# Sums of the second weight matrix given out singly over the groups of the first layer's last two units, in a fused pooling-attention and snake-activation kernel

## The chip, the cores and the metric

The kernel runs on one core of a Trainium2 chip. The metric is the device time of one execution in microseconds (us); the median of three executions before the change is 909.51 us (908.82 to 912.5). A core has a matrix engine (PE, with its weight loads PEld), a vector engine (DVE), an activation engine (ACT), GpSimd (POOL) and a queue engine (SP) that issues most transfers. Each engine works through its own instructions in the order in which the program recorded them, and waits for the others by semaphores.

## The reference

The attention pools keys and values by 8 and gives `x` of 4608 tokens by 512. What the change touches is behind it:

```python
def _moe_ref(x, w_in, w_out, alpha):
    h = x @ w_in                       # 4608x512 @ 512x2048
    s = np.sin(alpha * h)
    g = h + s * s / (alpha + 1e-09)
    return (g @ w_out)                 # 4608x2048 @ 2048x512
```

All of it is in 32-bit floats.

## The kernel before

**Two layers, one behind the other.** The first layer (`h` and `g`) runs over 9 units `u` of 512 tokens. Units 0 to 6 lie under the attention; units 7 and 8 are made by `hidden_late`, without attention beside them. `g` goes out to a buffer in HBM (`g_bridge`). The second layer (`outputs`) runs over 8 batches of 576 tokens and reads `g` back with `load_g` (tiles r11, r12, r21, r22).

**Seven products in place of eight.** Both layers use a Strassen-Winograd scheme: a product of two 2x2 block matrices is made from seven block products of sums of blocks. In the first layer a unit has four groups J = 0 to 3 (256 columns of each half of `h`); a group accumulates its products in PSUM banks b1, b6, b5, b7 (the name tells which product is the last or the first in it). Products 1 and 5 of groups 1 to 3 are themselves made by a second level of the scheme. That is `late_chain`: steps a, b, d, e for product 1 (c1) and for product 5 (c5). They are made for the *next* group N, in eight pieces, put between the halves of this group's products by `chain()`. Step a has two matmuls and two ACT copies (L1083 and L1084); d has one matmul and a DVE sum (L1093); e has two matmuls that wait for that DVE sum. Behind c1.e, `copy(N.b6, N.b1)` on ACT seeds bank b6 of the next group, and the next group's first product accumulates on it.

**Order inside a group** (J of 1 and above, L1158 to L1221): ACT sine of the group before (from b7); product 6 with c1.a and c5.a; copy b7 <- b6; squares of the group before; product 2 with c1.b and c5.b; the DVE sums that finish the group before (`finish`, L1224, one of 512 and one of 1024 columns) and its store; product 7 with c1.d, DVE sum g11 (L1102), c5.d; sine of it; product 3 with c1.e, DVE sum g01 (L1102), c5.e; sine and square of g01; DVE sum g00; product 4; copy of b5 to the tile p5 (L1221). Group 0 has the same products, but its chain starts a product later, so c1.e and c5.e fall into product 4, *behind* the sine and the square of g01 on ACT.

**The second layer's weights.** `load_w_out` brings `w_out` in four transfers, copies its quarters into seven tiles wb1 to wb7 on GpSimd (`put`, L704), and makes the outer sums on DVE (L713: 16 instructions of 128x512, four for each pair of row blocks). `inner_w` makes the sums of the scheme's second level (L731: four of 128x512 for each product 4, 6, 1, 2, 7, 5, and later 3); results land in `we1`, `we2` (which until then hold first-layer chain weights), or in the column blocks of the first layer's own weights `A[1]`, `A[2]`, `A[3]` that are used up. All are due before the second layer's product that reads them; product 1 is the first, then 2, 4, 6, 7, 5, 3.

**Where these are put.** A list `x[slot]` of 28 slots per unit (seven per group) holds what is recorded at a slot (`extras(k)`). `load_w_out` is a generator; `next(w)` at slots 9 to 23 of unit 7 and 6 to 20 of unit 8 each record a whole block: four L713 sums, or the four (twice: eight) L731 sums of a product. `late_weights` makes the chain weights of group J on GpSimd (L795), `late_x` the sums of x (L1066). `outputs` is a generator too: its first `next(o)` records the four DVE sums of 128x576 (L1454) that make the first operands of the second layer, the second its first product, the third its second product with an ACT copy (L1627) and two more sums.

Of the kernel before, what the change touches and what calls it, by code (L numbers as in the profile page):

```python
# [19 lines left out]
P = 128  # L20
# [20 lines left out]
class Kernel:  # L41
# [637 lines left out]
    def load_w_out(self, wp):  # L679

        nc, h, kk = self.nc, self.DM // 2, self.K2 // 2
        src = self.w_out.rearrange("(k p) n -> p k n", p=P)
        self.W = {}
        self.wb = {p: wp.tile([P, self.NJ, 2, 2, P], F32, name=f"wb{p}") for p in range(1, 8)}
        self.we = {p: wp.tile([P, 3, 2, 2, P], F32, name=f"we{p}") for p in (1, 2)}
        flat = lambda t: t[:].rearrange("p a b c d -> p (a b) (c d)")
        b11, b21, b22, t4, t1, t2, b12 = (flat(self.wb[p]) for p in range(1, 8))

        raw = {}
        for k in range(0, kk, 4):
            for i in range(2):
                t = self.wb[5 + i] if k == 0 else self.gp.tile([P, self.NJ, JW, 2, self.T], F32, name=f"r1{i + 1}")
                x = t[:].rearrange("p a b c d -> p (a b c d)")[:, 0:4 * self.DM]
                raw[i, k] = x.rearrange("p (k j a n c) -> p k j a n c", k=4, j=2, a=4, n=2)
                nc.sync.dma_start(out=x.rearrange("p (k c) -> p k c", k=4), in_=src[:, i * kk + k:i * kk + k + 4, :])

        def put(i, k):

            for j, t in enumerate(((b11, b12), (b21, b22))[i]):
                yield
                for n in range(2):
                    nc.gpsimd.tensor_copy(out=t[:, k:k + 4, n * P:(n + 1) * P].rearrange("p k (a c) -> p k a c", a=4),  # L704
                                   in_=raw[i, k][:, :, j, :, n, :])
        yield from put(0, 0)
        yield from put(1, 0)
        for c in range(0, kk, 2):
            if c == 2:
                yield from put(0, 4)  # L710
            yield
            s = slice(c, c + 2)
            tt = lambda o, x, y: nc.vector.tensor_tensor(out=o[:, s], in0=x[:, s], in1=y[:, s], op=OP.subtract)  # L713
            tt(t1, b12, b11)
            tt(t2, b22, t1)
            tt(b12, b22, b12)

            tt(t4, b21, t2)
            if c == 2:
                yield from put(1, 4)  # L720
        for p in (4, 6, 1, 2, 7):
            yield
            self.inner_w(p, wp)
        yield

    def inner_w(self, p, wp):

        nc = self.nc
        x = self.wb[p]
        b = lambda i, j: x[:, :, i - 1, j - 1, :].rearrange("p (k j) d -> p k j d", k=2)  # L730
        tt = lambda o, x, y: nc.vector.tensor_tensor(out=o, in0=x, in1=y, op=OP.subtract)  # L731
        if p in (4, 6, 7, 5):
            J = (4, 6, 7, 5).index(p)
            t1, t2, t4 = (self.A[i][:, :, J * JW * P:(J + 1) * JW * P].rearrange("p k (j d) -> p k j d", j=2) for i in (1, 2, 3))
        else:
            e = self.we[p] if p in self.we else wp.tile([P, 3, 2, 2, P], F32, name=f"we{p}")
            t1, t2, t4 = (e[:, i] for i in range(3))
        steps = [lambda: tt(t1, b(1, 2), b(1, 1)), lambda: tt(t2, b(2, 2), t1),
                 lambda: tt(b(1, 2), b(2, 2), b(1, 2)), lambda: tt(t4, b(2, 1), t2)]
        self.W[p] = {1: b(1, 1), 2: b(2, 1), 3: b(2, 2), 4: t4, 5: t1, 6: t2, 7: b(1, 2)}  # L740
        if wp:
            for f in steps:
                f()
        return steps

# [44 lines left out]
    def sums(self, steps):  # L792

        for o, x, y, op in steps:
            self.nc.gpsimd.tensor_tensor(out=o, in0=x, in1=y, op=op)  # L795
# [240 lines left out]
    def late_tiles(self, u):  # L1036

        if u < self.NU - 1:
            t = self.home(0, [P, self.K1, 2 * TH])
            t = [t[:, i] for i in range(4)]  # L1040
            m5 = self.we[2][:].rearrange("p a b c d -> p (a b c d)")[:, 1024:1280]
        else:
            t = [self.gq.tile([P, self.NJ, self.T], F32, name=f"s{i}0")[:].rearrange("p a b -> p (a b)")[:, 0:4 * P] for i in range(4)]
            m5 = self.gq.tile([P, self.NJ, self.T], F32, name="s01")[:].rearrange("p a b -> p (a b)")[:, 0:2 * P]
        self.m5 = m5.rearrange("p (a b c) -> p a b c", a=2, b=1)
        self.x2 = t[:2]
        self.w3 = [x.rearrange("p (i m) -> p i m", i=4) for x in t[2:]]

    def late_weights(self, J, ps=(1, 5)):

        for p in ps:
            n = (1, 5).index(p)
            w = self.w3[n] if J == 3 else self.we[J][:].rearrange("p a b c d -> p (a b c d)")[:, n * 512:n * 512 + 512].rearrange("p (i m) -> p i m", i=4)
            A = self.A[p][:].rearrange("p k (J j m) -> p k J j m", j=2, m=P)[:, :, J]
            L = lambda i, j: A[:, j, i]
            s1, s2, s3, s4 = (w[:, i] for i in range(4))
            self.sums(((s1, L(1, 0), L(1, 1), OP.add), (s2, s1, L(0, 0), OP.subtract), (s3, L(0, 0), L(1, 0), OP.subtract), (s4, L(0, 1), s2, OP.subtract)))
            self.WL[p, J] = {1: L(0, 0), 2: L(0, 1), 3: s4, 4: L(1, 1), 5: s1, 6: s2, 7: s3}

# [39 lines left out]
    def hidden_late(self, u, extra):  # L1099
# [20 lines left out]
        for J in range(self.NJ):  # L1120
            def extras(k):
                for f in extra[7 * J + k]:
                    f()
# [39 lines left out]
            if N:  # L1163
                y = self.psum([P, 4, P], N.banks[1])
                c1, c5 = (self.late_chain(N, p, ps, y[:, i:i + 2], i == 0) for p, ps, i in ((1, N.b1, 0), (5, N.b5, 2)))
                steps = iter((c1.a, c5.a, c1.b, c5.b, c1.d, c5.d, c1.e, c5.e))

            def chain():
                f = next(steps, None)
                if f:  # L1170
                    f()
                if N and f is c1.e:
                    copy(N.b6[:], N.b1[:])
            halves = (0, 1), (2, 3)
            behind = J == 0
            extras(2)
            product(G, 6, G.b6, halves[0])
            if not behind:
                chain()
# [19 lines left out]
            product(G, 7, G.b7, halves[1])  # L1199
            add(G.g[:, 1, :, 1], G.b7[:], G.p5[:])  # L1200
            chain()
            sin(G, 1, 1, G.g[:, 1, :, 1])
            extras(5)
            product(G, 3, G.b6, halves[0])
# [1 line left out]
            product(G, 3, G.b6, halves[1])  # L1206
            add(G.g[:, 0, :, 1], G.b6[:], G.p5[:])
            chain()
            sin(G, 0, 1, G.g[:, 0, :, 1])
            square(G, 0, 1)  # L1210
            add(G.g[:, 0, :, 0], G.b1[:], G.s[:, 0, :, 0])
            extras(6)
            product(G, 4, G.b7, halves[0])
            if behind:
                chain()
            product(G, 4, G.b7, halves[1])
            if behind:
                chain()
            if N:
                N.p5 = self.tp.tile([P, JW, TH], F32, name="p5")  # L1220
                nc.vector.tensor_copy(out=N.p5[:], in_=N.b5[:])  # L1221
# [227 lines left out]
    def outputs(self):  # L1449
# [136 lines left out]
        for k in range(len(seq) + 1):  # L1586
# [47 lines left out]
            if last:  # L1634
                if k != 1:
                    second()
                third()
                if k == 5:
                    self.inner_w(3, self.gs)
                combine(last)  # L1640
            for _ in sums:
                pass
# [9 lines left out]
    def run(self):  # L1652
        nc, tc = self.nc, self.tc
        pool = lambda s, n, b, **kw: s.enter_context(tc.tile_pool(name=n, bufs=b, **kw))
        with ExitStack() as top:
# [10 lines left out]
            with ExitStack() as one:  # L1666
# [35 lines left out]
                for u in range(self.NU):  # L1702
                    x = self.carry(u)
                    if u == self.B - 1:
# [1 line left out]
                        wo = pool(top, "wo", 1, side="right")  # L1706
                        self.gp = pool(top, "gp", 1, side="right")
                        self.WL, self.XL = {}, {}
                        w = self.load_w_out(wp=wo)
                        next(w)  # L1710
                        self.late_tiles(u)
                        for i in (9, 10, 12, 13, 15, 16, 17, 18, 20, 21, 23):
                            x[i].append(lambda: next(w))
                        self.late_weights(1, (1,))
                        self.late_x(u, 1)
                        x[0].append(lambda: self.late_weights(1, (5,)))
                        x[1].append(lambda: self.late_x(7, 5, nc.vector))
                        x[4].append(lambda: self.late_weights(2))
                        x[6].append(lambda: self.late_weights(3))
                    elif u > self.B - 1:  # L1720
                        homes.close()
                        self.gq = pool(top, "gq", 1, side="right")
                        self.late_tiles(u)
                        for i in (6, 10, 14, 15, 17, 20):
                            x[i].append(lambda: next(w))
                        x[0].append(lambda: self.late_x(8, 1))
                        x[0].append(lambda: self.late_x(8, 5))
                        x[6].append(lambda: self.late_weights(3))
                        x[5].append(lambda: self.load_g(0, ("r11", "r12", "r22")))
                        for i, f in zip((23, 25, 25, 27), self.inner_w(5, None)):  # L1730
                            x[i].append(f)
                        o = self.outputs()
                        for i in (22, 25, 27):
                            x[i].append(lambda: next(o))
                    (self.hidden if u < self.B - 1 else self.hidden_late)(u, x)
                self.end_hidden()
# [41 lines left out]
```

## Time and profile before

| what | value |
|---|---|
| median of three executions | 909.51 us (908.82 to 912.5) |
| profiled execution, its own time | 911.08 us |
| span of its instructions | 909.3 us |
| granted TensorE clock | 0.999 |
| unit 7 (419.4 to 468.7 us) | 49.3 us |
| unit 8, with the first matmuls of the second layer (468.7 to 526 us) | 57.3 us |
| DVE busy in unit 7 / in 468.7 to 526 | 32.01 us / 46.70 us |
| POOL busy in unit 7 / in 468.7 to 526 | 22.02 us / 7.81 us |
| behind it (526 to 909.3 us) | second layer |

The profile's timeline lists instructions by start time; equal ones that follow each other are merged, so that "x4" with 1.03 us is the time of four matmuls together. In brackets stands the idle time of the engine ahead of the instruction and which engine's instruction ended it. Times in the text, such as 494.23, are us from the start of the span.

### The profile page before, as it was taken

The page shows a single profiled execution, that of the slowest core. Times are in us where ns is not written, and L with a number is a line of the kernel's source. Part 1 is how long each engine was busy: PE and PEld are TensorE (multiplying, and loading weights), DVE is VectorE, ACT ScalarE, POOL GpSimd, SP SyncE. Part 2 cuts the span into 40 slices and gives each one's busy share as a digit, 9 for nine tenths or more (in the row PEclk, how much of TensorE's full clock was granted, in tenths as well). Part 3 has the DMA queues.
Part 4 walks back from the last instruction along what each step waited for, and adds up shares of the span by engine and source line. Part 5 has one row for each costly group of instructions (what it writes and reads, how often), then busy time and mean ns, then how long its engine had stood idle before and what let it go on. Part 6 is the DMA issues. An engine that isn't in the chain of part 4 may idle for free.

```text
span 909.3 us, 18214 instructions
## 1 busy us (share of the span) xinstructions
PE 895.6 (98%) x7086; PEld 816.1 (90%) x7086; DVE 691.8 (76%) x1035; ACT 444.1 (49%) x1082; POOL 243.9 (27%) x276
## 2 busy tenths in 40 slices
PE   8999999999999999999999899999999999999997
PEld 5787888888888888888888799999999999999997
DVE  6675766758677685765577999979798888889894
ACT  5696685877768778687767621111121111111111
POOL 4788462824428253436330000000000000000000
PEclk9999999999999999999999999999999999999999
DMA  9956766759577595648136247161618162534401
GB/s 248 252 179 170 198 187 188 202 144 259 151 210 189 172 237 138 178 142 294 49 124 216 93 117 226 36 216 39 223 27 222 40 186 77 169 92 128 134 14 40
DMA packets 128749, 141.15 MB, mean 155 GB/s; under 512 B 46920, under 2 KB 95704, under 8 KB 128664
## 3 DMA queue, kind: packets, MB, share of 16 engines
q1 hardware_dynamic: 125880, 137.88, 53.2%
q10 hardware_dynamic: 2784, 2.11, 0.9%
q8 instruction: 56, 0.92, 0.5%
q14 instruction: 29, 0.24, 0.1%
HBM read 75.37 MB, written 47.19 MB: 135 GB/s over the span
## 4 chain that ended last, share of the span: by engine, by line
PE 91%; DVE 3%; ACT 2%; POOL 1%; DMA 1%; issue 1%; SPq 0%; DVEq 0%; POOLq 0%
PE PS L1499 42%; PE PS L835 33%; PE PS L1117 6%; PE PS L1015 3%; PE PS L308 2%; PE PS L600 2%; PE PS L1079 1%; PE PS L613 1%; DMA q<-in_q_dram 1%; POOL kvin L131 1%; DMA h<-in_k_dram 1%; ACT s L992 1%; DVE h L1224 1%; DVE h L1102 0%; ACT s L985 0%
## 5 line engine op out<-in xcount | busy, mean ns | idle before, releaser
L835 PE MATMUL PS<-home,a 128*128 128x256 f32 x848 | 199.9, 382 | 1.8 <-DVE h L810 1.3
L835 PEld LDWEIGHTS PS<-home,a 128*128 128x128 f32 x848 | 156.7, 190 | 28.7 <-issue 5.0
L835 PE MATMUL PS<-home,as 128*128 128x256 f32 x576 | 138.9, 383 | 0.0
L1499 PE MATMUL PS<-s,wb 128*128 128x144 f32 x896 | 119.2, 286 | 0.7 <-ACT PS L1627 0.7
L835 PEld LDWEIGHTS PS<-home,as 128*128 128x128 f32 x576 | 105.2, 190 | 14.8 <-ACT PS L811 1.2
L1549 POOL TENSOR_TENSOR cc<-cc,cb 128x576 f32<-128x576 f32 x1 | 2.0, 1980 | 423.2 <-DVE cb L1454 423.2
L1499 PEld LDWEIGHTS PS<-s,wb 128*128 128x128 f32 x896 | 113.6, 190 | 1.1 <-ACT PS L1627 1.1
L992 ACT ACTIVATE s<-s,c 128x256 f32<-128x256 f32 (+1 forms) x228 | 114.2, 565 | 0.0
L131 POOL TENSOR_TENSOR kvin<-kvin 96x768 f32<-96x768 f32 (+3 forms) x42 | 73.6, 1752 | 72.3 <-DMA kvin<-in_v_dram 70.6
L985 ACT ACTIVATE s<-h,al 128x256 f32<-128x256 f32 x144 | 65.5, 509 | 51.0 <-DVE h L810 30.5
L1627 ACT COPY PS<-PS 128x144 f32<-128x144 f32 x56 | 14.7, 263 | 144.3 <-PE PS L1499 141.7
L1499 PE MATMUL PS<-r,wb 128*128 128x144 f32 x512 | 73.2, 286 | 0.0
L1499 PE MATMUL PS<-s,a 128*128 128x144 f32 x512 | 73.2, 286 | 0.0
L810 DVE TENSOR_TENSOR h<-PS,p 128x512 f32<-128x512 f32 x56 | 38.1, 680 | 44.6 <-PE PS L835 28.3
L985 ACT ACTIVATE s<-PS,al 128x256 f32<-128x256 f32 x144 | 59.9, 467 | 16.0 <-PE PS L835 13.9
L1499 PEld LDWEIGHTS PS<-r,wb 128*128 128x128 f32 x512 | 67.1, 190 | 0.1
L1499 PEld LDWEIGHTS PS<-s,a 128*128 128x128 f32 x512 | 67.0, 190 | 0.0
L1224 DVE TENSOR_TENSOR h<-PS,s 128x512 f32<-128x512 f32 x36 | 24.7, 686 | 51.4 <-ACT s L992 51.4
L1647 ACT COPY PS<-PS 128x144 f32<-128x144 f32 x56 | 14.7, 263 | 88.0 <-PE PS L1499 88.0
L1224 DVE TENSOR_TENSOR h<-h,s 128x1024 f32<-128x1024 f32 x36 | 55.4, 1538 | 0.9 <-ACT s L992 0.9
L1499 PE MATMUL PS<-x,wb 128*128 128x144 f32 x384 | 54.9, 286 | 0.0
L1499 PE MATMUL PS<-s,we 128*128 128x144 f32 x384 | 54.9, 286 | 0.0
(274 smaller groups left out, 1662.7 us busy)
## 6 DMA issues: line engine op xcount, KB each, us to landing
g_bridge<-h SPq DMA_DIRECT2D x72, 512.0 KB
r<-g_bridge SPq DMA_DIRECT2D x31, 1152.0 KB
out_dram<-o SPq DMA_DIRECT2D x122, 72.0 KB
kvin<-in_k_dram SPq DMA_DIRECT2D x14, 576.0 KB
q<-in_q_dram SPq DMA_DIRECT2D x7, 1024.0 KB
kvin<-in_v_dram SPq DMA_DIRECT2D x14, 512.0 KB
aM<-tr SPq DMA_DIRECT2D x54, 92.0 KB
aM<-tr SPq DMA_DIRECT2D x54, 88.0 KB
```

The source lines that it names most:

```text
L131: self.nc.gpsimd.tensor_tensor(out=t[..., 0:w] if w > D else out, in0=t[..., 0:w], in1=t[..., w:2 * w], op=OP.add)
L308: nc.tensor.matmul(ps[e][r0 + r:r0 + r + q.shape[-1], h, :], q[s], kb[s, hp, :], start=True, stop=True)
L600: nc.tensor.matmul(o[r:r + 64], w, x, start=start and i < 2, stop=False, skip_group_check=True)
L810: add = lambda o, x, y: nc.vector.tensor_tensor(out=o, in0=x, in1=y, op=OP.add)
L835: nc.tensor.matmul(ps[:, jj, :], self.A[p][:, kk, f * P:(f + 1) * P], x[:, kk, :], start=(start and n == 0), stop=(kk == 1), skip_group_ch ...
L985: self.nc.scalar.activation(out=G.s[:, i, jj, j, :], in_=src[:, jj], func=AF.Sin, scale=self.al[:, f:f + 1])
L992: self.nc.scalar.activation(out=x, in_=x, func=AF.Square, scale=self.c[:, f:f + 1])
L1015: nc.tensor.matmul(o, W[m][:, G.J - J0], X[m], start=start and n == 0, stop=True, skip_group_check=True)
L1117: nc.tensor.matmul(ps[:, jj, :], self.A[p][:, kk, f * P:(f + 1) * P], x[:, kk, :], start=(start and n == 0), stop=(kk == 1), skip_group_ch ...
L1224: add = lambda o, x, y: self.nc.vector.tensor_tensor(out=o, in0=x, in1=y, op=OP.add)
L1499: nc.tensor.matmul(out, W[:, J // 2, J % 2, :], A[:, J, :], start=(start and J == 0), stop=(J == self.NJ - 1), skip_group_check=True)
L1627: nc.scalar.copy(out=x1[:, 0, :], in_=x0[:, 1, :])
```

## The change

- `load_w_out` no longer is a generator: it returns `put` and `sums`, and `inner_w` returns its four sums as functions. They are recorded one by one by a new `fill(n)` in `hidden_late`, which stands at three places of each group: n = 0 ahead of product 6, n = 1 behind c5.d (behind the sum g11, ahead of its sine), n = 2 at the end of product 4.
- The GpSimd copies `put` move up: the first half from slots 9 to 13 of unit 7 to slot 2, ahead of `late_weights(2)` (which moves from slot 4 to 3) and `late_weights(3)`; the second half to slot 6.
- The eight inner sums of products 1 and 2 go to GpSimd.
- In group 0 the sine and square of g01 are recorded behind the last two chain steps, and so behind the seed copy of b6 on ACT. In group 3 (no N), `extras(6)` moves ahead of that sine, and with it the ACT copy L1627.
- The first `next(o)` moves from slot 22 of unit 8 (group 3) to `fill(1)` of group 1. For this the tiles that lay in its way move: the chain's m5 into a used block of `A[5]`, unit 8's chain weights of group 3 into used blocks of `A[6]` and `A[7]`; `late_weights(3)` of unit 8 therefore waits for product 6 and 7 of group 0.

```diff
+        def sums(c):
             s = slice(c, c + 2)
-            tt = lambda o, x, y: nc.vector.tensor_tensor(...)
+            tt = lambda o, x, y: lambda: nc.vector.tensor_tensor(...)
+            return [tt(t1, b12, b11), tt(t2, b22, t1), tt(b12, b22, b12), tt(t4, b21, t2)]
+        return put, sums
...
-        tt = lambda o, x, y: nc.vector.tensor_tensor(out=o, in0=x, in1=y, op=OP.subtract)
+        eng = nc.gpsimd if p in (1, 2) else nc.vector
+        tt = lambda o, x, y: eng.tensor_tensor(out=o, in0=x, in1=y, op=OP.subtract)
...
+            self.m5 = self.A[5][:, :, 0:P].unsqueeze(2)
+            self.w3 = [self.A[i][:, :, 0:2 * P].rearrange("p k (j m) -> p k j m", j=2) for i in (6, 7)]
...
+            def fill(n):
+                for f in self.fillers[u, J, n]:
+                    f()
...
             extras(2)
+            fill(0)
             product(G, 6, G.b6, halves[0])
...
             add(G.g[:, 1, :, 1], G.b7[:], G.p5[:])
             chain()
+            fill(1)
             sin(G, 1, 1, G.g[:, 1, :, 1])
...
             add(G.g[:, 0, :, 1], G.b6[:], G.p5[:])
             chain()
-            sin(G, 0, 1, G.g[:, 0, :, 1])
-            square(G, 0, 1)
+            if not N:
+                extras(6)
+            if not behind:
+                sin(G, 0, 1, G.g[:, 0, :, 1])
+                square(G, 0, 1)
             add(G.g[:, 0, :, 0], G.b1[:], G.s[:, 0, :, 0])
-            extras(6)
+            if N:
+                extras(6)
             product(G, 4, G.b7, halves[0])
...
             if behind:
                 chain()
+                sin(G, 0, 1, G.g[:, 0, :, 1])
+                square(G, 0, 1)
+            fill(2)
...
+                        x[2] += [lambda: put(0, 0), lambda: put(1, 0)]
+                        x[3].append(lambda: self.late_weights(2))
                         x[6].append(lambda: self.late_weights(3))
+                        x[6] += [lambda: put(0, 4), lambda: put(1, 4)]
+                        self.fillers[7, 1, 0] = sums(0) + sums(2)[:2]
+                        self.fillers[7, 1, 1] = sums(2)[2:]
+                        self.fillers[7, 2, 0] = sums(4)
+                        self.fillers[7, 3, 0] = sums(6)
...
+                        w = {p: self.inner_w(p, q) for p, q in ((1, self.we[1]), (2, self.we[2]), (4, 0), (6, 1), (7, 2), (5, 3))}
                         o = self.outputs()
+                        F = self.fillers
+                        F[8, 0, 2] = w[4]
+                        F[8, 1, 0] = w[1] + w[6][:1]
+                        F[8, 1, 1] = w[6][1:3] + [lambda: next(o)]
+                        F[8, 2, 0] = w[6][3:] + w[2] + w[7][:1]
+                        F[8, 2, 1] = w[7][1:3]
+                        F[8, 3, 0] = w[7][3:] + w[5][:1]
+                        F[8, 3, 1] = w[5][1:3]
+                        F[8, 3, 2] = w[5][3:]
```

More of the change, by code (lines that the diff above doesn't have):

```diff
@@ L701, in put, with inner_w @@
             for j, t in enumerate(((b11, b12), (b21, b22))[i]):
-                yield
                 for n in range(2):
                     nc.gpsimd.tensor_copy(out=t[:, k:k + 4, n * P:(n + 1) * P].rearrange("p k (a c) -> p k a c", a=4),
[L705 to L711, printed above, removed]
-            s = slice(c, c + 2)
[L713 to L726, printed above, removed]
+                                          in_=raw[i, k][:, :, j, :, n, :])
+        def sums(c):
+            s = slice(c, c + 2)
+            tt = lambda o, x, y: lambda: nc.vector.tensor_tensor(out=o[:, s], in0=x[:, s], in1=y[:, s], op=OP.subtract)
+            return [tt(t1, b12, b11), tt(t2, b22, t1), tt(b12, b22, b12), tt(t4, b21, t2)]
+        return put, sums
+    def inner_w(self, p, parts):
         nc = self.nc
@@ L730, in inner_w @@
         b = lambda i, j: x[:, :, i - 1, j - 1, :].rearrange("p (k j) d -> p k j d", k=2)
-        tt = lambda o, x, y: nc.vector.tensor_tensor(out=o, in0=x, in1=y, op=OP.subtract)
-        if p in (4, 6, 7, 5):
-            J = (4, 6, 7, 5).index(p)
-            t1, t2, t4 = (self.A[i][:, :, J * JW * P:(J + 1) * JW * P].rearrange("p k (j d) -> p k j d", j=2) for i in (1, 2, 3))
-        else:
[L736 to L739, printed above, removed]
+        eng = nc.gpsimd if p in (1, 2) else nc.vector
+        tt = lambda o, x, y: eng.tensor_tensor(out=o, in0=x, in1=y, op=OP.subtract)
+        if isinstance(parts, int):
+            t1, t2, t4 = (self.A[i][:, :, parts * JW * P:(parts + 1) * JW * P].rearrange("p k (j d) -> p k j d", j=2) for i in (1, 2, 3))
+        else:
+            t1, t2, t4 = (parts[:, i] for i in range(3))
         self.W[p] = {1: b(1, 1), 2: b(2, 1), 3: b(2, 2), 4: t4, 5: t1, 6: t2, 7: b(1, 2)}
[L741 to L744, printed above, removed]
+        return [lambda: tt(t1, b(1, 2), b(1, 1)), lambda: tt(t2, b(2, 2), t1),
+                lambda: tt(b(1, 2), b(2, 2), b(1, 2)), lambda: tt(t4, b(2, 1), t2)]
     def bank(self, shape, i=None):
@@ L1042, in late_tiles @@
         else:
-            t = [self.gq.tile([P, self.NJ, self.T], F32, name=f"s{i}0")[:].rearrange("p a b -> p (a b)")[:, 0:4 * P] for i in range(4)]
-            m5 = self.gq.tile([P, self.NJ, self.T], F32, name="s01")[:].rearrange("p a b -> p (a b)")[:, 0:2 * P]
+            t = [self.gq.tile([P, self.NJ, self.T], F32, name=f"s{i}1")[:].rearrange("p a b -> p (a b)")[:, 0:4 * P] for i in range(2)]
+            self.m5 = self.A[5][:, :, 0:P].unsqueeze(2)
+            self.x2 = t
+            self.w3 = [self.A[i][:, :, 0:2 * P].rearrange("p k (j m) -> p k j m", j=2) for i in (6, 7)]
+            return
         self.m5 = m5.rearrange("p (a b c) -> p a b c", a=2, b=1)
@@ L1055, in late_weights @@
             L = lambda i, j: A[:, j, i]
-            s1, s2, s3, s4 = (w[:, i] for i in range(4))
+            s1, s2, s3, s4 = (w[:, i] for i in range(4)) if len(w.shape) == 3 else (w[:, i // 2, i % 2] for i in range(4))
             self.sums(((s1, L(1, 0), L(1, 1), OP.add), (s2, s1, L(0, 0), OP.subtract), (s3, L(0, 0), L(1, 0), OP.subtract), (s4, L(0, 1), s2, OP.subtract)))
@@ L1638, in outputs @@
                 if k == 5:
-                    self.inner_w(3, self.gs)
+                    for f in self.inner_w(3, self.gs.tile([P, 3, 2, 2, P], F32, name="we3")):
+                        f()
                 combine(last)
@@ L1708, in run @@
                         self.WL, self.XL = {}, {}
-                        w = self.load_w_out(wp=wo)
-                        next(w)
+                        put, sums = self.load_w_out(wp=wo)
                         self.late_tiles(u)
-                        for i in (9, 10, 12, 13, 15, 16, 17, 18, 20, 21, 23):
-                            x[i].append(lambda: next(w))
                         self.late_weights(1, (1,))
@@ L1717, in run @@
                         x[1].append(lambda: self.late_x(7, 5, nc.vector))
-                        x[4].append(lambda: self.late_weights(2))
+                        x[2] += [lambda: put(0, 0), lambda: put(1, 0)]
+                        x[3].append(lambda: self.late_weights(2))
                         x[6].append(lambda: self.late_weights(3))
+                        x[6] += [lambda: put(0, 4), lambda: put(1, 4)]
+                        self.fillers = defaultdict(list)
+                        self.fillers[7, 1, 0] = sums(0) + sums(2)[:2]
+                        self.fillers[7, 1, 1] = sums(2)[2:]
+                        self.fillers[7, 2, 0] = sums(4)
+                        self.fillers[7, 3, 0] = sums(6)
                     elif u > self.B - 1:
@@ L1723, in run @@
                         self.late_tiles(u)
-                        for i in (6, 10, 14, 15, 17, 20):
-                            x[i].append(lambda: next(w))
                         x[0].append(lambda: self.late_x(8, 1))
@@ L1729, in run @@
                         x[5].append(lambda: self.load_g(0, ("r11", "r12", "r22")))
-                        for i, f in zip((23, 25, 25, 27), self.inner_w(5, None)):
-                            x[i].append(f)
+                        w = {p: self.inner_w(p, q) for p, q in ((1, self.we[1]), (2, self.we[2]), (4, 0), (6, 1), (7, 2), (5, 3))}
                         o = self.outputs()
-                        for i in (22, 25, 27):
+                        F = self.fillers
[7 more added lines that the diff above has]
+                        F[8, 3, 2] = w[5][3:]
+                        for i in (25, 27):
                             x[i].append(lambda: next(o))
```

## The prediction

> **What bounds the kernel now.** I read the page first, then who waited for whom from 419.4 to 526 us (units 7 and 8), then the timeline there. The page says that PE is the bound: whatever is gained has to come out of its few gaps.
>
> ```profile
> PE 895.6 (98%) x7086; PEld 816.1 (90%) x7086; DVE 691.8 (76%) x1035; ACT 444.1 (49%) x1082; POOL 243.9 (27%) x276
> ```
>
> In the list of waits for that stretch (engine and line, what it waited for: total us, times, longest) the gaps of PE stand with their causes:
>
> ```profile
> PEld PS L1079 <- DVE PS L1093: 2.9, 2, 1.6
> ...
> PEld PS L1499 <- ACT PS L1627: 1.1, 1, 1.1
> ...
> PEld PS L1117 <- ACT PS L1103: 0.7, 2, 0.4
> ...
> PEld PS L1117 <- DVE h L1102: 0.7, 1, 0.7
> ```
>
> That is six gaps. I size each from the timeline by the start of the matmul behind it less where it would have started at the pace of its neighbours: sixteen 256-column matmuls' loads take 3.43 us, so one step is (3.43 - 0.19)/15 = 0.216; a 128-column one is 0.109, a 144-column one 0.122. c1.e of group 2, unit 7: 456.52 - (454.55 + 4 x 0.216) = 1.10. The same in unit 8: 505.85 - 504.52 = 1.33. Seed copies: 435.21 - 434.88 = 0.33 and 484.31 - 483.98 = 0.33. Product 4 of unit 8's last group: 518.94 - 518.30 = 0.64; behind L1627: 521.65 - 520.77 = 0.88. The first matmul behind each takes 0.10 longer than the step. So the most that can be won is 4.61 + 0.6 = 5.2 us of 909.
>
> **The change part by part.** *Spreading the sums.* The gap at 456.52 comes from four L713 sums (453.51 to 456.1) ahead of L1093 on DVE, the one at 505.85 from twelve L731 sums (496.04 to 503.7), the one at 518.94 from two L731. In the new DVE order nothing stands ahead of L1093 in those groups but p5, one to four sums that run while `finish` waits for ACT anyway (2.16 us idle before 451.77), and `finish`. So I take off 1.20, 1.43 and 0.74. The copy L1627 goes ahead of a sine and a square: 0.98 off.
>
> *Seed copies.* c1.e ends at 433.74, so the copy can run at 433.76 instead of 434.58, and PE's 0.43 goes. But the pair sine and square then lies behind it: ACT works from 433.76 through copy 0.52, sine 0.82, square 0.79, sine 0.82 to 436.71, then L1083 and L1084 (0.27 + 0.28), and c5.a, which waits for L1084, starts at about 437.30; before, it started at 437.41. What was taken from one wait comes back two steps on: 0.1 off for each of the two, not 0.43.
>
> *GpSimd.* Its own time is known from the same shape: 1.27 us for 128x512, eight are 10.2 us, with POOL idle there (7.81 busy of 57.3), and we1 and we2 are due at 517.3 or later.
>
> ```profile
> L675 POOL TENSOR_TENSOR as<-a,a 128x512 f32<-128x512 f32 x4 | 5.1, 1271 | 5.1 <-DMA a<-in_moe_w_in_dram 5.1
> ```
>
> But the trace shows what a GpSimd sum does to a DVE sum with both inputs in SBUF beside it. Here four DVE sums of 128x512 meet POOL sums of 128x128 (start, us, engine, line):
>
> ```profile
> 90.28 0.45 POOL L795 TENSOR_TENSOR last<-home 128x128 f32<-128x128 f32 x1 [3.03 <-DVE home L805]
> 90.30 0.97 DVE L805 TENSOR_TENSOR home<-home,home 128x512 f32<-128x512 f32 x1
> 90.81 0.78 POOL L795 TENSOR_TENSOR last<-home,last 128x128 f32<-128x128 f32 x1
> ...
> 91.20 0.94 DVE L805 TENSOR_TENSOR home<-home 128x512 f32<-128x512 f32 x1
> ...
> 91.56 0.90 POOL L795 TENSOR_TENSOR last<-home 128x128 f32<-128x128 f32 x1
> ...
> 92.06 0.94 DVE L805 TENSOR_TENSOR home<-home,home 128x512 f32<-128x512 f32 x1
> 92.42 0.90 POOL L795 TENSOR_TENSOR last<-home,last 128x128 f32<-128x128 f32 x1
> ```
>
> They take turns: a pair every 0.86 us, where DVE alone steps by 0.61 (L713) and POOL alone by 0.41. A DVE sum at 219.06 took 2.28 instead of 1.22 beside a POOL sum of 1.27. So beside POOL's 128x512 a pair should step by 0.86 + (1.24 - 0.41) = 1.7 us. DVE sums that read PSUM (L1102, L1224's first, L1221) never lengthen.
>
> The Trainium skill says the same more sharply (SBUF — State Buffer, on the shared port pair): the pair is an exclusive lock held for the whole instruction, so that the loser waits out all of it; it speaks against handing sums to GpSimd while DVE is dense. By it a pair would be a full 1.27 + 0.65 = 1.9 us.
>
> *Where the GpSimd sums fall.* The first four (product 1) wait for c1.e and c5.e of group 0, 482.2 to 484.1: exactly when `fill(2)` records product 4's four on DVE. Those last 4 x 1.7 = 6.8 in place of 2.6. The other four (product 2) wait for c1.e of group 1, and run beside `fill(1)`.
>
> *`fill(1)` of group 1, unit 8: the place that decides.* Before, DVE has this gap in it, and ACT follows on what stands behind:
>
> ```profile
> 492.45 0.42 DVE L1093 TENSOR_TENSOR PS<-PS,s 128x256 f32<-128x256 f32 x1
> ...
> 494.23 0.69 DVE L1102 TENSOR_TENSOR h<-PS,p 128x512 f32<-128x512 f32 x1 [1.37 <-PE PS L1117]
> ...
> 494.96 0.91 ACT L985 ACTIVATE s<-h,al 128x256 f32<-128x256 f32 x2 [1.01 <-DVE h L1102]
> ...
> 495.77 0.89 ACT L992 ACTIVATE s<-s,c 128x256 f32<-128x256 f32 x2
> ...
> 496.57 0.81 ACT L985 ACTIVATE s<-PS,al 128x256 f32<-128x256 f32 x2
> ...
> 497.71 0.36 ACT L1083 COPY PS<-PS 128x256 f32<-128x256 f32 x1 [0.33 <-PE PS L1079]
> ...
> 497.98 0.27 ACT L1084 COPY s<-PS 128x128 f32<-128x128 f32 x1
> 498.31 0.30 PEld L1079 LDWEIGHTS PS<-home,as 128*128 128x128 f32 x2 [0.17 <-ACT s L1084]
> ```
>
> The gap is 1.36 us; two L731 (1.30) and four L1454 sums (511.80 to 514.66: 2.86) now go into it, 4.2 us alone. Behind them in DVE's queue waits g01, behind g01 the sine, square, sine, L1083 and L1084 on ACT, and behind L1084 PE's c5.a: it starts 3.76 us after g01 does (0.73 + 0.81 + 0.80 + 0.82 + 0.27 + 0.33). r11 is no wait: its load is issued at 475.47 and landed by 483.7.
>
> *The sum.* Unit 7: seed -0.1; the six sums of `fill(0)` of group 1 meet the second half of the GpSimd copies (0.56 each, a pair at about 1.0): they end at 441.7 rather than 439.6, `finish` at 443.5 and g01's chain 0.7 late (between 0, if copies do not meet DVE sums, and 0.7; I take it, as both read SBUF); gap at 456 -1.2. Unit 8 so starts at -0.6. Product 4's sums end at 489.0, p5 489.6, one sum 490.3, `finish` 492.1, L1093 492.5: c1.e at 492.55, c5.d's sum ends 493.5. `fill(1)`: first DVE sum behind a POOL sum at 494.8, three more pairs to 499.9, two more sums to 501.25; g01 starts there, c5.a at 505.0 in place of 498.38: +6.7 with its slow first matmul. Then -1.43, -0.74, -0.98: **+3.5 us**. The profiled execution would be 914.6; its 911.08 is 1.6 above the median of the runs, so against that median 913.0.
>
> No other edit costs anything. The moved copies find `w_out` landed (by my reading of the landings at 420.8 and 423.5 for the first two), and chain weights of group 2 are ready at about 432 where c1.a wants them at 435.9; without that cover each us late would be a us of PE. Unit 8's group-3 weights, now behind product 7 of group 0, end near 479 and are wanted at 496.9. SP issues the same transfers in the same order; POOL has no queue of them.
>
> **Rivals.** *DVE keeps its turn* (for it: at 32.45 two L805 ran back to back and a POOL sum waited for both, 2.07 instead of 1.0; against it: the turns above). Then unit 8 is at -1.4 at group 1, g01 starts at 491.5 + 4.2 = 495.7, c5.a at 499.4, +1.0, less 3.15: -2.1, 907.4. Even this can't reach the 5.2, since 4.2 us don't fit in 1.36.
> *Full price* (slower): a POOL sum keeps DVE out for all its 1.27, a pair is 1.92: `fill(2)` 0.9 longer, `fill(1)` 0.9 longer, +5.3: 914.8. It decides from a pair of 1.83 on. For it: 2.28 at 219.06; against: 0.86 is 0.15 below the sum of both steps.
> *The spreading fails too*: the gaps at 504 and 518 to 521 come back because DVE is still late in groups 2 and 3: +3.5 + 3.15 = +6.7, 916.2. Against it: group 2 has three DVE sums at `fill(0)` and two at `fill(1)`, 1.3 in a gap of 1.36.
> *All gaps close*: -5.2, 904.3; only if g01 isn't held as I say.
>
> **How the numbers follow.** Turns at about 1.7: 0.55; DVE keeps its turn: 0.17; full price: 0.15; spreading fails: 0.08; all close: 0.05. About 0.5% (4.55 us) is what a measurement of this kernel can tell from no change, so the first case, good to some 1.5 us, lies mostly within: of its 0.55 I give 0.17 to slower. Slower 0.17 + 0.15 + 0.08 = 0.40, faster 0.05, same 0.55. Range: from -2.1 (907) to +6.7 (916.5).
>
> **What would show it.** Right: at c5.a of group 2 in unit 8 PE waits for ACT L1084's successor some 6 to 7 us, DVE's two-input sums there last 1.3 to 1.9 us, POOL's beside them too; the four gaps behind it and the one at 456 are gone; second layer as long as before. Wrong: DVE sums of 0.68 beside POOL's, or no wait at c5.a.

## The result and the profile after

The changed kernel takes 913.34 us (median of 19 runs, 911.05 to 915.78) against 909.26 us for the kernel before (19 runs, 908.1 to 912.5): the ratio is 1.0045 (95% interval 1.0036 to 1.0054), so it is 4.1 us slower. Forecast were 913.0 us and +3.5 us.

In the changed kernel the lines have other numbers: the matmuls L1117 are now L1102, the chain's matmuls L1079 are L1064 and its second copy L1084 is L1069, its sum L1093 is L1078, g11 and g01 (L1102) are L1087, the seed copy L1103 is L1088, the inner sums L731 are L719, the first operands L1454 are L1452, p5 and `finish` are L1219 and L1222, the copy L1627 is L1625.

The page's first line says that PE is still the bound; its busy time is up by 1.7 us and its share is the same:

```profile
PE 897.3 (98%) x7086; PEld 817.5 (90%) x7086; DVE 696.3 (76%) x1027; ACT 444.0 (49%) x1082; POOL 260.4 (29%) x284
```

The list of waits of the changed kernel from 418 to 526 us (engine and line, what it waited for: total us, times, longest) shows which gaps of PE are left:

```profile
PEld PS L1064 <- DVE h L1087: 5.3, 1, 5.3
...
PEld PS L1064 <- ACT as L1069: 1.3, 3, 0.7
...
PEld PS L1064 <- DVE PS L1078: 1.2, 2, 0.6
```

The waits for the seed copy, for L1087 ahead of product 4 and for the copy L1625 are gone from it, and those for the chain's sum have shrunk from 1.6 to 0.6 us at most. In their place stands one wait of 5.3 us, for g01 (5.3 counted on the weight loads, 4.9 on the matmuls). The timeline of DVE shows what g01 had ahead of it in group 1 of unit 8 (start, us, engine, line):

```profile
491.07 0.42 DVE L1078 TENSOR_TENSOR PS<-PS,as 128x256 f32<-128x256 f32 x1
491.40 1.60 DVE L719 TENSOR_TENSOR a<-wb,a 128x512 f32<-128x512 f32 x1
492.92 1.75 DVE L719 TENSOR_TENSOR wb<-wb 128x512 f32<-128x512 f32 x1
494.60 1.82 DVE L1452 TENSOR_TENSOR s<-r 128x576 f32<-128x576 f32 x1
496.45 1.70 DVE L1452 TENSOR_TENSOR s<-s,r 128x576 f32<-128x576 f32 x1
498.07 0.75 DVE L1452 TENSOR_TENSOR s<-r 128x576 f32<-128x576 f32 x1
498.74 0.74 DVE L1452 TENSOR_TENSOR s<-r,s 128x576 f32<-128x576 f32 x1
499.41 0.68 DVE L1087 TENSOR_TENSOR h<-PS,p 128x512 f32<-128x512 f32 x1
```

The timeline of POOL beside it:

```profile
491.18 1.27 POOL L719 TENSOR_TENSOR we<-wb 128x512 f32<-128x512 f32 x1 [4.45 <-PE PS L1064]
492.56 1.57 POOL L719 TENSOR_TENSOR we<-wb,we 128x512 f32<-128x512 f32 x1
494.09 1.71 POOL L719 TENSOR_TENSOR wb<-wb 128x512 f32<-128x512 f32 x1
495.76 1.78 POOL L719 TENSOR_TENSOR we<-wb,we 128x512 f32<-128x512 f32 x1
```

Four pairs, in turns: DVE steps by 1.52, 1.68, 1.85 and 1.62 us while POOL is at work, and by 0.67 as soon as it is done (498.07, 498.74). POOL pays too: the same 128x512 sum takes 1.57 to 1.78 where the first, alone for its first 0.2 us, takes 1.27. And on PE, in its timeline:

```profile
494.20 1.03 PE L1102 MATMUL PS<-home,as 128*128 128x256 f32 x4
500.14 0.80 PE L1064 MATMUL PS<-home,a 128*128 128x128 f32 x2 [4.92 <-DVE h L1087]
...
501.16 1.91 PE L1102 MATMUL PS<-home,as 128*128 128x256 f32 x4
503.06 0.80 PE L1064 MATMUL PS<-home,as 128*128 128x128 f32 x2
```

The matmuls at 500.14 are c1.a of group 2, those at 503.06 c5.a. Four matmuls of 256 columns take 1.03 us at 494.20 and 1.91 at 501.16: behind the wait PE is slow. The table of windows gives the granted clock (stretch and length; busy us and number of instructions of PE, PEld, DVE, ACT and POOL; then PEclk, DMA share and GB/s):

```profile
494.80:498.40 3.60, 0.42 (x2) 0.02 (x1) 3.57 (x3) 0.00 (x0) 2.74 (x2) 1.00 0.00 0
498.40:500.10 1.70, 0.00 (x0) 0.00 (x0) 1.70 (x4) 0.00 (x0) 0.00 (x0) 0.68 0.00 0
500.10:503.06 2.96, 2.92 (x8) 2.03 (x8) 2.38 (x4) 2.89 (x8) 0.00 (x0) 0.50 0.00 0
503.06:505.70 2.64, 2.64 (x9) 2.37 (x9) 0.00 (x0) 1.95 (x5) 0.00 (x0) 0.50 0.00 0
505.70:508.00 2.30, 2.30 (x15) 2.06 (x14) 1.82 (x2) 1.31 (x4) 0.00 (x0) 0.97 0.00 0
```

**Where the time went.** Both programs have 7086 matmuls in the same order, so the start of the n-th in one trace less its start in the other is a running account. At 420 us, ahead of the change, it stands at -1.35: two executions differ by that much where the programs are the same, and I count from there. At 460 it is -0.93 (unit 7's gain), at 490 it is -1.14, at c5.a +6.03, behind the slow matmuls at 505 it is +7.44, and the three gaps that are gone take off 1.43, 0.75 and 0.98: **+4.28**, constant from 530 us to the end. The second layer itself has not changed.

### The profile page after: what moved, and what is told of

Its sections match the earlier page's. It is cut to its first block, busy times and chain, and to the rows that moved or that the text cites. A ratio compares the mean times of both kernels' runs of the same rounds, so it can differ in the third digit from the quotient of the medians.

```text
span 911.9 us, 18225 instructions
## 1 busy us (share of the span) xinstructions
PE 897.3 (98%) x7086; PEld 817.5 (90%) x7086; DVE 696.3 (76%) x1027; ACT 444.0 (49%) x1082; POOL 260.4 (29%) x284
## 4 chain that ended last, share of the span: by engine, by line
PE 49%; DVE 3%; issue 0%; DVEq 0%
PE PS L1497 42%; PE PS L1102 5%; PE PS L1064 1%; DVE a L719 1%; DVE wb L709 1%; DVE s L1452 1%; DVE wb L719 0%; DVE h L1222 0%; DVE h L1087 0%; DVE as L719 0%; DVE PS L1078 0%; DVE p L1219 0%; DVE o L1519 0%; DVE cc L1452 0%; DVEq L1087 0%
## 5 line engine op out<-in xcount | busy, mean ns | idle before, releaser
L1625 ACT COPY PS<-PS 128x144 f32<-128x144 f32 x56 | 14.7, 263 | 145.2 <-PE PS L1497 142.6
L1222 DVE TENSOR_TENSOR h<-PS,s 128x512 f32<-128x512 f32 x36 | 24.7, 685 | 52.3 <-ACT s L974 52.3
L1222 DVE TENSOR_TENSOR h<-h,s 128x1024 f32<-128x1024 f32 x36 | 54.9, 1524 | 0.9 <-ACT s L974 0.9
```

The lines of the kernel that those rows point to most:

```text
L1222: add = lambda o, x, y: self.nc.vector.tensor_tensor(out=o, in0=x, in1=y, op=OP.add)
L1625: nc.scalar.copy(out=x1[:, 0, :], in_=x0[:, 1, :])
```

## The experiments

All but e4 start from the changed kernel. "In the trace" means this running account against the kernel before, from 420 us to the end.

**e1: first operands back in group 3.**

```diff
-                        F[8, 1, 1] = w[6][1:3] + [lambda: next(o)]
+                        F[8, 1, 1] = w[6][1:3]
...
-                        for i in (25, 27):
+                        for i in (22, 25, 27):
```

> The changed kernel with one thing undone: the first operands of the second layer (four DVE sums of 128x576) go back to slot 22, group 3 of unit 8; everything else of the change stays, the eight sums on GpSimd too. Theory A (those four sums, contended by GpSimd, in a gap of 1.4 us are what holds g01): only two contended sums (about 3.3 us) remain there, PE's 5.1 us wait at c1.a of group 2 falls under 0.5 us, the half clock behind it (500.1 to 505.7) goes too, and the time falls by about 8 us from the changed kernel's 913.3 to 905.3 (904 to 907). Theory B (GpSimd's contention as such makes DVE late in unit 8, wherever the four sums stand): a wait of over 2 us stays in groups 1 to 3, 909 or more. Theory C (the spreading doesn't pay, DVE is late again in group 3 with the four sums back there): the wait moves to 510 to 520 us and the time is 907 to 910.

Measured: 906.5 us, ratio 0.9973 (0.9957 to 0.9989), in the trace -1.87. The 5.1 us and the half clock are gone, and nothing comes back in group 3, which is against C and against the 909 of B. But a wait is left that I had not expected. DVE:

```profile
490.36 1.59 DVE L719 TENSOR_TENSOR a<-wb,a 128x512 f32<-128x512 f32 x1
491.87 1.75 DVE L719 TENSOR_TENSOR wb<-wb 128x512 f32<-128x512 f32 x1
493.55 0.68 DVE L1087 TENSOR_TENSOR h<-PS,p 128x512 f32<-128x512 f32 x1
```

and PE in the same kernel:

```profile
494.28 0.49 PE L1064 MATMUL PS<-home,a 128*128 128x128 f32 x2
...
497.20 0.49 PE L1064 MATMUL PS<-home,as 128*128 128x128 f32 x2 [1.35 <-ACT as L1069]
```

g01 is soon enough for c1.a, nearly, but not for c5.a, which waits for the sine, square, sine and two copies on ACT behind g01. My expectation had looked at the first of the two only.

**e2: all inner sums on DVE**, the first operands in group 1 as in the changed kernel.

```diff
-        eng = nc.gpsimd if p in (1, 2) else nc.vector
+        eng = nc.vector
```

> The changed kernel with the eight inner sums of products 1 and 2 on DVE in place of GpSimd; the four sums of 128x576 stay in group 1. Theory A: product 4's sums take 0.65 each in place of 1.7 (DVE some 4 us earlier there, but four sums of product 1 of 0.6 come in ahead of finish), the sums behind c5.d take 4.2 us in place of 8.0, g01 is some 2 to 3 us late in place of 5, and, if PE's clock only halves behind a wait of some length, that goes as well: gaps of about 4 us in all against 5.9 before, 907 to 908. Theory B (contention is nearly all of the loss): no wait over 1 us at c1.a of group 2, 905 or less. Theory D (four sums in a gap of 1.4 us cost as much without GpSimd, or eight sums ahead of product 6 of group 2 make the next wait): 910 or more.

Measured: 906.68 us, ratio 0.9968 (0.9958 to 0.9979), in the trace -2.18. DVE does eight sums more and yet is earlier: product 4's four sums step by 0.6 to 0.7, and g01 starts at 493.17 in place of 499.41. The waits on PE in 480 to 520 us:

```profile
PE PS L1064 <- ACT as L1069: 1.3, 1, 1.3
PE PS L1064 <- DVE h L1087: 0.3, 1, 0.3
```

The clock is 1.0 throughout. This is A's mechanism at less than its price: c5.a is 2.05 us late, and PE's idle time from 400 to 560 us comes to 1.8 us (5.4 in the changed kernel), where A had about 4. B fails by its time, 905 or less. Its other sign did come, since c1.a waits 0.3 us only; the wait of more than 1 us, without any contention, stands at c5.a, where neither theory had looked. D fails too.

**e3: both edits.**

> Both edits together: first operands back in group 3, all inner sums on DVE. Theory A: no wait over 0.6 us in groups 1 and 2, 904.5 to 906; at most 1 us below the kernel that only moves the operands back, since GpSimd's contention costs PE next to nothing once the four sums are away. Theory B: 2 us or more below that kernel. Theory C: a wait in group 2 or 3 of over 1 us since DVE now carries all sums, 907 or more.

Measured: 904.48 us, ratio 0.9943 (0.9927 to 0.9959), in the trace -4.31: the lowest median of this study, and 5 us below the kernel before. The list of PE's waits from 419 to 520 us has one line left, the chain's sum in unit 7:

```profile
PE PS L1064 <- DVE PS L1078: 0.2, 1, 0.2
```

and DVE now waits for PE ahead of g01, not PE for it:

```profile
491.87 0.69 DVE L1087 TENSOR_TENSOR h<-PS,p 128x512 f32<-128x512 f32 x1 [0.17 <-PE PS L1102]
```

A holds for the waits and the time; its "at most 1 us below" e1 does not: it is 2.0 (2.4 in the trace), which is B's number. A had priced the contention too low: the contended sums that are left in e1 (product 4's four and two in `fill(1)`) made c5.a 1.9 us late, and c1.e of group 1 half a microsecond. So each theory had one part of it. Set side by side, in us against the kernel before (from the ratios, times 909.3):

| | inner sums 1, 2 on GpSimd | on DVE |
|---|---|---|
| first operands in group 1 | +4.1 (the change) | -2.9 (e2) |
| in group 3 | -2.5 (e1) | -5.2 (e3) |

Either undone alone is worth some 7 us, the other one then only 2 to 3 more: the turns cost per DVE sum, so they cost most where the change puts most sums, and only with both together is PE's wait long enough for the half clock (4.92 us, against 1.35 at most in e1 and e2).

**e4: the seed copy's order alone**, put into the kernel before.

```diff
-            sin(G, 0, 1, G.g[:, 0, :, 1])
-            square(G, 0, 1)
+            if not behind:
+                sin(G, 0, 1, G.g[:, 0, :, 1])
+                square(G, 0, 1)
...
             if behind:
                 chain()
+                sin(G, 0, 1, G.g[:, 0, :, 1])
+                square(G, 0, 1)
```

> The kernel before with one part of the change alone: in group 0 the sine and square of g01 behind the last two chain steps, so the seed copy of b6 goes ahead of them. Theory A: PE's gap behind the seed copy (0.33 + 0.10, in units 7 and 8) goes, and a wait of 0.2 to 0.35 comes at c5.a of group 1, as sine and square are late: 0.1 to 0.2 net each. Rival: the gap goes with nothing in its place, 0.43 each. The two are told apart by the gaps at 434 to 438 and 483 to 487 us, not by the time.

Measured: 909.86 us in one run, in the trace -0.43 for the two units together. The wait at the seed copy is gone, and the one for c5.a, two steps on, has grown from 0.17 to 0.38:

```profile
436.39 0.30 PEld L1079 LDWEIGHTS PS<-home,as 128*128 128x128 f32 x2 [0.38 <-ACT we L1084]
```

0.21 for each unit, so A: a half of 0.43 comes back.

**e5: the copy L1625 back behind the sine and square**, from e3.

```diff
-            if not N:
-                extras(6)
             if not behind:
                 sin(G, 0, 1, G.g[:, 0, :, 1])
                 square(G, 0, 1)
             add(G.g[:, 0, :, 0], G.b1[:], G.s[:, 0, :, 0])
-            if N:
-                extras(6)
+            extras(6)
```

> From the kernel with both edits (904.5, all large gaps gone), one part of the change undone: in group 3 the extras with the copy L1625 go back behind the sine and square of g01. Theory A: the gap of 0.88 + 0.10 us ahead of the second layer's matmuls of the copy comes back in unit 8's end, alone, about 905.5. Rival: the earlier first operands already cover it, no gap there; the reorder was not needed.

Measured: 904.86 us in one run, in the trace -3.96, 0.35 above e3. The wait that comes back (this kernel's L1622 is the copy):

```profile
PEld PS L1494 <- ACT PS L1622: 0.5, 1, 0.5
```

The gap is 0.23 + 0.10, neither the 0.98 of A nor nothing. Of the 0.98 in the kernel before, about 0.35 hung on this order. I put the rest down to the spreading: in the kernel before, ACT stood 3.90 us until 518.92 for g11, which DVE did late, behind its sums, and the sines and squares of g11 and g01 lay between that and the copy at 521.33. In e5 it is DVE that waits for PE ahead of g11 (0.71 us, at 510.96). No run undoes the spreading alone.

**e6 and e7: four and eight more DVE sums ahead of g01, no GpSimd.** From e2; the sum t2 of product 6 is recorded five or nine times, each time from the same operands.

```diff
-                        F[8, 1, 1] = w[6][1:3] + [lambda: next(o)]
+                        F[8, 1, 1] = 5 * w[6][1:2] + w[6][2:3] + [lambda: next(o)]
```

> All inner sums on DVE, first operands in group 1 as in the changed kernel, and one of product 6's sums there (t2) recorded five times instead of once: 4 x 0.60 = 2.4 us more DVE work ahead of g01, GpSimd idle. It measures how a late g01 turns into time, and whether the half clock comes from the length of the wait. Theory A: c1.a's wait grows one to one, from 0.44 to 2.85 us, the wait at c5.a stays 1.5, PE stays at full clock behind waits this short: 906.7 + 2.4 = 909.1. Rival (the clock goes down behind any wait of this kind, or a wait that ACT covers grows less than one to one): half clock for some us and 910.5 or more, or under 908.

> The same with the sum recorded nine times: 4.8 us more DVE work, so c1.a's wait would be 5.25 us, as long as in the changed kernel, but with GpSimd idle. Theory A (the length of PE's idle time halves the clock, nothing else): a granted clock of 0.5 for some us behind the wait, c5.a's wait shrinks from 1.5 to about 0.4 as the slow matmuls ahead of it take its time, and 1 to 3 us of slow matmuls behind c5.a: 911.5 + 1.3 = 912.8 (912 to 914.5). Rival (the half clock of the changed kernel came from something else, such as contention with GpSimd): clock stays 1.0, c5.a still waits 1.5, 911.5.

Measured: e6 910.71 us, ratio 1.0015 (1.0001 to 1.003), in the trace +1.21; e7 913.93 us, ratio 1.005 (1.0033 to 1.0066), in the trace +3.65. Each repeat writes over what the one before it wrote and steps by 0.727 us, not 0.60, so 2.9 and 5.8 us were added. PE's wait at c1.a is 3.19 us in e6 and 6.09 in e7:

```profile
498.23 0.49 PE L1064 MATMUL PS<-home,a 128*128 128x128 f32 x2 [3.19 <-DVE h L1087]
```

```profile
501.24 0.79 PE L1064 MATMUL PS<-home,a 128*128 128x128 f32 x2 [6.09 <-DVE h L1087]
```

The windows of e6 (columns as above, PEclk third from last):

```profile
494.90:498.20 3.30, 0.14 (x1) 0.00 (x0) 3.27 (x6) 0.00 (x0) 0.00 (x0) 1.00 0.00 0
498.20:499.00 0.80, 0.77 (x5) 0.77 (x6) 0.80 (x2) 0.79 (x2) 0.00 (x0) 0.84 0.00 0
499.00:501.15 2.15, 1.71 (x5) 0.81 (x3) 2.12 (x4) 2.15 (x8) 0.00 (x0) 0.50 0.00 0
```

and of e7:

```profile
495.00:499.00 4.00, 0.15 (x1) 0.00 (x0) 3.86 (x7) 0.00 (x0) 0.00 (x0) 0.80 0.00 0
499.00:501.20 2.20, 0.00 (x0) 0.00 (x0) 2.20 (x5) 0.00 (x0) 0.00 (x0) 0.50 0.00 0
501.20:504.20 3.00, 2.96 (x9) 2.06 (x9) 2.96 (x5) 2.89 (x8) 0.00 (x0) 0.50 0.00 0
504.20:506.00 1.80, 1.80 (x12) 1.70 (x13) 1.80 (x4) 1.66 (x5) 0.00 (x0) 1.00 0.00 0
```

The half clock comes without any GpSimd work, so contention is not its cause. In e6 I was wrong for this execution: 3.2 us of wait were enough. There the half clock cost 0.48 us in the trace (1.21 against e2's -2.18, less the 2.91 put in). It did not come in every execution of e6, as the clocks further down show. In e7 the clock was back at 504.2, just when c5.a could start (504.17), so in this execution it cost nothing; the expected 1.3 us are not in this trace.

**e8: unit 7 spread further**, from e3.

```diff
-                        self.fillers[7, 1, 0] = sums(0) + sums(2)[:2]
-                        self.fillers[7, 1, 1] = sums(2)[2:]
-                        self.fillers[7, 2, 0] = sums(4)
-                        self.fillers[7, 3, 0] = sums(6)
+                        self.fillers[7, 1, 0] = sums(0)[:2]
+                        self.fillers[7, 1, 1] = sums(0)[2:]
+                        self.fillers[7, 2, 0] = sums(2)
+                        self.fillers[7, 2, 1] = sums(4)[:2]
+                        self.fillers[7, 3, 0] = sums(4)[2:] + sums(6)[:2]
+                        self.fillers[7, 3, 1] = sums(6)[2:]
```

> From the kernel with both edits, unit 7's outer sums spread further: two in fill(0) and two in fill(1) of group 1, four and two in group 2, four and two in group 3, in place of six, two, four, four. Theory A: the gap of 0.38 + 0.10 at c1.e of group 1, unit 7, comes from six DVE sums that meet the GpSimd copies ahead of finish; with two there it goes, and 0.5 us is won: 904.0. Rival: the gap comes from finish waiting for ACT, and stays.

Measured: 905.27 us, ratio 0.9955 (0.994 to 0.997), in the trace -4.79, 0.48 below e3. DVE in the changed kernel had `finish` right behind six sums:

```profile
434.34 5.61 DVE L709 TENSOR_TENSOR wb<-wb,wb 128x512 f32<-128x512 f32 x6
439.87 0.68 DVE L1222 TENSOR_TENSOR h<-PS,s 128x512 f32<-128x512 f32 x1
440.47 1.58 DVE L1222 TENSOR_TENSOR h<-h,s 128x1024 f32<-128x1024 f32 x1
```

In e8 it waits for ACT instead, and c1.e does not wait any more:

```profile
439.32 0.69 DVE L1222 TENSOR_TENSOR h<-PS,s 128x512 f32<-128x512 f32 x1 [2.52 <-ACT s L974]
```

So A by the trace. The times of e3 and e8 can't tell half a microsecond; either is some 4 to 5 us faster than the kernel before.

## Why the prediction was right, and where its terms were off

The mechanism is the one forecast; the sum was +3.5 where the trace has +4.28 and the medians +4.1. Term by term, in us against the kernel before (negative is won):

| term | forecast | measured |
|---|---|---|
| seed copies, each unit | -0.1 | -0.21 |
| c1.e of group 1, unit 7 (GpSimd copies beside the six sums) | +0.7 | +0.48 |
| gap at 456 | -1.20 | -1.20 |
| step of a pair, DVE beside POOL | 1.7 | 1.65 (four of product 4: 6.60 in all), 1.67 (in `fill(1)`) |
| c5.a of group 2, unit 8, behind g01 by | 3.76 | 3.65 |
| c5.a late by, in all | +6.7 | +6.03 |
| half clock behind c5.a | not seen | +1.41 |
| three gaps behind | -3.15 | -3.16 |

*What decides.* That g01's delay reaches PE through ACT at c5.a is the step that carried the forecast, and the five kernels where PE waits there confirm it. Take c5.a's due time as the start of product 6's first four matmuls plus 0.87 plus 1.31 (c1.a and the four matmuls between, from e3, where nothing waits):

| kernel | g01 starts | c5.a starts | difference | c5.a due | late |
|---|---|---|---|---|---|
| change | 499.41 | 503.06 | 3.65 | 496.38 | 6.68 |
| e1 | 493.55 | 497.20 | 3.65 | 495.33 | 1.87 |
| e2 | 493.17 | 496.83 | 3.66 | 494.78 | 2.05 |
| e3 | 491.87 | 496.02 | 4.15 | 496.02 | 0 |
| e6 | 497.49 | 501.15 | 3.66 | 496.19 | 4.96 |
| e7 | 500.50 | 504.17 | 3.67 | 496.31 | 7.86 |

Wherever g01 is late, the difference is 3.65 to 3.67 us, and e6 and e7 grow by just the 2.91 and 5.82 us that were put in. e3, with no wait, shows 4.15, so g01 has half a microsecond to spare there.

*The first sign would have been different.* "PE waits for ACT L1084's successor some 6 to 7 us" at c5.a was not what the list of waits shows: PE stood 4.92 us at c1.a, for g01 itself, and only 0.4 for ACT at c5.a. Two things make this so. c1.a needs g01 as well, 1.3 us earlier in PE's order, which I had overlooked; and the half clock stretched the matmuls between the two from 1.31 to 2.92 us, which hid most of ACT's part. The sum was not harmed, because c5.a's start follows from g01 alone.

*The missing term.* Nothing in the prediction asked what a wait of 5 to 7 us does to PE's clock. It cost 1.41 us in the profiled execution, more than the +0.78 by which the sum was short; that c5.a was 0.6 less late than forecast (unit 7 gained 0.93 in place of 0.6, ACT's chain was 0.11 shorter, and pairs of 1.65 took less) made up for half of it. The right size therefore came in part from two errors of opposite sign, which is luck.

*No change or slower.* The prediction gave 0.55 to no change and 0.40 to slower, since it took 0.5% as what a measurement of this kernel can tell. With 19 runs of each kernel the interval reaches 0.09% to either side, so these 0.45% are clearly a slowdown.

*The rivals.* "DVE keeps its turn" (907.4) fell: DVE's sums beside POOL took 1.60 to 1.82, not 0.68 to 0.75. "Full price", deciding from a pair of 1.83 on, fell: 1.65 to 1.67 on the mean of each place, though one pair of the four in `fill(1)` stepped by 1.85; the Trainium skill's rule (SBUF — State Buffer, on the shared port pair) of a lock for the whole instruction was too dear by 0.25 us a pair here. "The spreading fails too" fell: no gap behind 506 us. "All gaps close" fell for the change but is nearly what e3 does: -4.31 of the 5.2 that were to be won.

*One term right in its size, but not in its cause*: the 0.98 at the second layer's matmuls came off, yet e5 shows that the order of the copy on ACT is worth 0.35 of it.

*How often the clock falls.* The account above is of one execution of each kernel, but the mean granted clock is on record for each execution. 6.8 us at half clock take 0.5 x 6.8/912 = 0.0037 off that mean. It is 0.996 or less in 14 of the changed kernel's 19 executions (0.997 or 0.998 in the other five), in all four of e7 and in five of e6's ten. It is never under 0.997 in the 40 executions of the kernel before that ran beside the experiments, nor in the 36 of e1, e2, e3 and e8. So the half clock goes with the long wait and is no accident of one execution. In e6, whose wait is the shortest of the three, four executions show 0.999, with a median of 909.4 us against 911.8 for the five at 0.996 or less: there the same edit brought the half clock in some executions and not in others.

What stays open is how much of the slow time PE pays for in other executions. By the traces it was 1.41 us in the changed kernel, 0.48 in e6 and nothing in e7. The median of e7 is 7.2 us above that of e2, where 5.8 us were put in, but the two were measured on different chips, and by the intervals of their ratios the difference can be anything from 5.7 to 9.2.

## What to carry to other kernels

Before work is put into an engine's idle time ahead of an instruction, ask by when that instruction is due, over every consumer: here the idle time was 1.36 us and the slack behind it half a microsecond (4.15 - 3.65 in e3), read off at the consumer two engines on. Giving sums to GpSimd made DVE later here than doing them itself: DVE did eight sums more in e3 than in e1, and neither c1.e of group 1 nor c5.a of group 2 waited any more. Where a change turns several short waits into a long one, price the clock behind it too.

## What the runs showed of the hardware

**A PE that stands still for some microseconds comes back at half clock.** Waits of 0.3 and 1.35 us (e1, e2) leave the granted clock at 1.0. Behind 3.19, 4.92 and 6.09 us of wait (the profiled executions of e6, the change, e7) it is 0.50. By the windows it stays there for 3.4 us in e6 (498.74 to 502.16) and for 6.8 in the changed kernel (499.0 to 505.83) and in e7 (497.36 to 504.19): once or twice the same 3.4 us (the ends are worked out from windows of half a microsecond). It began 3.7 us after PE's last matmul had ended in e6, half a microsecond *after* PE was at work again; 3.8 us after it in the changed kernel; and 2.2 us after it in e7. So its start isn't tied to the start of the wait. The Trainium skill says so (TensorE: Matmul & The Clock Gate, Part 1: a free-running window of about 3.4 us, half clock behind an idle one); the lengths agree. But if the window ends where the clock falls, PE was at work in a part of it in e6, where 2.9 us of it were idle, and in e7, where 2.2 us were: it need not be idle as a whole. How much is enough no run shows.

**Both partners of a contended pair pay.** POOL's 128x512 sum went from 1.27 us to between 1.57 and 1.78 beside DVE's two-input sums, DVE's 128x512 sum from 0.68 to between 1.59 and 1.76; together they take 1.65 a pair, where one behind the other they would be 1.27 + 0.60 = 1.87.
